# TensorE branches on each expert's token count: the last 64 rows of second parts left out where they are empty

## The chip, the cores and the metric

The kernel runs on one core of a Trainium2 chip. The metric is the device time of one execution in microseconds. PE is TensorE's matmul side and PEld its weight load, DVE is VectorE, ACT ScalarE, POOL GpSimd, SP SyncE. A letter q behind an engine's name (PEldq, SPq) marks what its sequencer does itself: branches, register loads, waits, DMA issues.

## What is computed

Three stages follow each other, in float32 from outside: a gated linear attention, a mixture of eight experts of which each token uses two, and a dense layer. Cut to what matters:

```python
# attention, per batch (4) and head (8), 768 steps, head size 48
state = f[:, :, t, :, None] * state + np.einsum('bhd,bhe->bhde', k[:, :, t], v[:, :, t])
y[:, :, t] = np.einsum('bhd,bhde->bhe', q[:, :, t], state)
# experts: 3072 tokens, 384 wide, 8 experts, 1024 hidden
logits = x @ w_gate
noisy_logits = logits + np.log1p(np.exp(x @ w_noise)) * noise
top2 = np.argpartition(-noisy_logits, 2, axis=1)[:, :2]
for e in range(E):
    for k in range(2):
        mask = top2[:, k] == e
        h = np.maximum(x[mask] @ w1[e], 0.0)
        out[mask] += top2_w[mask, k, None] * (h @ w2[e])
# dense: 2048 hidden
h = x @ w_in
return ((h - np.tanh(h)) @ w_out).astype(np.float32)
```

## The kernel before

Each expert has room for 832 tokens (CAP): the rows of its tokens are scattered to slots in DRAM (`xs`), the slots are loaded transposed (`load_x`), and two products run over them. The slots above an expert's token count are filled with zeros and computed all the same.

An expert's 832 slots are two parts, whose sizes `blocks(e)` gives: 320 and 512 for experts 0 and 7, 384 and 448 for expert 1, 512 and 320 for the others. Below, (5,1) is the second part of expert 5 and (5,0) its first. The hidden width is cut in eight, so a part has eight steps f. One step of a part is:

- `first_products`: nine matmuls with 128 hidden rows as the stationary side and the part's n tokens as moving columns (float16 high and low halves, three products for each of three 128-wide pieces of the input). The result, `ph`, is one PSUM bank.
- `moe_first` then lets ACT take the relu of it (hs, high half) and DVE the low half.
- `second_products`, two steps later (LAG = 2): for each 128 tokens of the part three matmuls with hs as the stationary side and 384 moving columns, into the banks b0, b1, b2, b5 (py). A rest of 64 tokens takes two matmuls, since its high and low halves stand side by side (`if m == 64`).
- after the last step `moe_second` lets ACT and DVE copy py out, and SP stores the rows to DRAM (`y_rows`).

The order of parts is written out by hand (`order`): (0,0) (1,0) (2,0) (0,1) (1,1) (2,1) (3,0) (3,1) (4,0) (4,1) (5,0) (5,1) (6,0) (7,0) (6,1) (7,1). In the trace (0,1) begins at 189 us, (2,1) at 249, (3,0) at 270, (5,1) at 403, (6,1) at 476, (7,1) at 496; the dense layer begins at 530. The main loop runs over n, the steps of all parts in that order, and puts other work in each step: weights of coming experts are loaded (`load_weights`) and split into high and low halves (`split_weights`, L155 on ACT and L156 on DVE), the dense layer's weights are decoded, the sums of squares of the weights are taken for a check (`weight_sum`, L161, on ACT: two per step in second parts), tokens of the first rows of the dense layer are gathered (`gather_y`, POOL) and combined. Each engine works off its own instructions in program order. At the end a flag decides whether a general fallback runs: every engine loads it (L1222) and branches on it (L1223); in the run shown the fallback's body is jumped over.

Of the kernel before, what the change touches and what calls it, by code (L numbers as in the profile page):

```python
# [26 lines left out]
FILLED = 640  # L27
Y_EARLY = (NE - 1) * CAP + 320


def blocks(e):
    cut = {0: 320, 1: 384, NE - 1: 320}.get(e, 512)
    return (0, cut), (cut, CAP - cut)


EARLY = {(0, 0): 12, (1, 0): 16, (2, 0): 20}
CLEARED = 16


# [35 lines left out]
def fast(ctx, tc, flag, f_cols, kq_cols, v_rows, gates, blank, void, w12, w_in, w_out, out):  # L75
# [102 lines left out]
    def load_x(e, blk, pieces):  # L178
        if pieces.start == 0:
            new_xt((e, blk))  # L180
        at, n = blocks(e)[blk]
        lo, hi = pieces.start * 128, min(n, pieces.stop * 128)
        if lo >= hi:
            return
        t = nc.sync.dma_start_transpose(XT[e, blk][:, :, lo:hi], xs[e * CAP + at + lo:e * CAP + at + hi, :])
        if (e, blk) in EARLY:
            early_rows[e, blk].append(t)
            for o in scatters[2 * EARLY[e, blk]:]:
                tc.declare_no_dep(t.ins, o.ins, reason="slots of late tokens are clamped to later rows")
# [7 lines left out]
    HS, PY = {}, {}  # L197
    def first_products(ph, n, lhs, key):
# [7 lines left out]

    def second_products(key, f, last, rhs, parts):
        hs = HS.pop((key, f))
        wh, wl = (w.rearrange("p a b -> p (a b)") for w in rhs)
        for i, (c0, m) in enumerate(parts):  # L210
            if f == 0:
                PY[key, i] = bank(f"py{i}", ("b0", "b1", "b2", "b5")[i])[:, :DM]
            p = PY[key, i]
# [7 lines left out]

    def moe_first(e, blk, f):
        n = blocks(e)[blk][1]
        w = RING[e, f]
        ph = bank("ph", next(tags["ph"]))
        first_products(ph, n, lambda a: (w[:, 0, a, :], w[:, 1, a, :]), (e, blk))
        hs = tiles.tile([128, 1024], F16, name="hs", bufs=4)
# [12 lines left out]

    def moe_second(e, blk, f):
        w = RING[e, f]
        second_products((e, blk), f, 7, (w[:, 0, 3:6, :], w[:, 1, 3:6, :]), parts(e, blk))
        if f < 7:
            return
        for i, (c, n) in enumerate(parts(e, blk)):
# [10 lines left out]
            nc.sync.dma_start(y_rows[at:at + n, :], y[:n])  # L257

    def pace(t):
        nc.gpsimd.tensor_copy(spacer, t)  # L260
# [9 lines left out]
    def moe_products(n):  # L270
        if n < len(moe_steps):
            moe_first(*moe_steps[n])
        if n >= LAG:
            moe_second(*moe_steps[n - LAG])

# [523 lines left out]
    def ff_second(blk, f):  # L799
        w = RING[NE, f // 2]  # L800
        c = 3 * (f % 2)
        second_products(("m", blk), f, 15, (w[:, 0, c:c + 3, :], w[:, 1, c:c + 3, :]),
                        [(128 * i, 128) for i in range(4)])
# [17 lines left out]
    for n in range(4, len(moe_steps) + LAG):  # L821
# [79 lines left out]
    def checks():  # L901
# [15 lines left out]
        nc.vector.tensor_scalar(total[:, 4:5], count[:, 4, NE - 1:NE], 320.0, None, op0=OP.is_le)  # L917
        holds(2, count[:, 0], float(CAP), OP.is_le)
# [363 lines left out]
```

## Time and profile before

| what | us |
|---|---|
| median of 3 runs | 910.54 (910.02 to 911.67) |
| the profiled execution | 914.9 |
| its span | 913.1 |
| PE busy | 896.9 |
| ACT busy | 604.7 |
| DVE busy | 576.8 |

The page's engine busy times are sums over the span; a matmul record is longer than the distance to the next one, as matmuls overlap in the array, so distances between starts tell what a matmul costs. The chain of waits follows the last instruction back to whatever released it.

### The profile page before, as it was taken

How to read it: one execution, taken by the hardware profiler on the slowest of the kernel's cores; microseconds unless marked ns; L12 is line 12 of the kernel's file. 1: busy time of each engine (PE TensorE's matmuls, PEld its weight loads, DVE VectorE, ACT ScalarE, POOL GpSimd, SP SyncE). 2: the span in 40 equal slices, each digit the busy share in tenths (PEclk: the TensorE clock that was granted, in tenths of full speed). 3: DMA queues.
4: the chain of work that ended last, by engine and by line, in shares of the span. 5: the costliest groups of instructions: out<-in, count | busy, mean ns of one | idle time of the engine just before them, and what ended most of it. 6: DMA issues, size and time to landing. Idle time of an engine off the chain costs nothing.

```text
span 913.1 us, 17400 instructions
## 1 busy us (share of the span) xinstructions
PE 896.9 (98%) x6422; PEld 531.0 (58%) x6422; DVE 576.8 (63%) x1167; ACT 604.7 (66%) x1560; POOL 173.8 (19%) x240
## 2 busy tenths in 40 slices
PE   8999899999999999999999999999999999999996
PEld 7888765555565656555566555555555555555553
DVE  7988866633467555666766756566465565565764
ACT  7989766455686656768658766666666666666652
POOL 3588834100000000000002132031140220320000
PEclk9999999999999999999999999999999999999999
DMA  8989999731568574646645722032031230330101
GB/s 246 204 256 288 277 283 313 215 99 53 153 199 217 136 190 116 181 126 170 159 137 121 191 71 61 10 96 44 18 98 25 61 70 10 79 58 4 36 1 39
DMA packets 112318, 116.58 MB, mean 128 GB/s; under 512 B 68208, under 2 KB 91376, under 8 KB 112080
## 3 DMA queue, kind: packets, MB, share of 16 engines
q1 hardware_dynamic: 105792, 96.11, 39.7%
q0 software_dynamic: 6144, 18.88, 7.0%
q8 instruction: 52, 0.85, 0.4%
q14 instruction: 42, 0.34, 0.1%
q10 hardware_dynamic: 288, 0.39, 0.1%
HBM read 72.88 MB, written 30.38 MB: 113 GB/s over the span
## 4 chain that ended last, share of the span: by engine, by line
PE 89%; DMA 5%; ACT 3%; issue 1%; DVE 1%; SPq 1%; POOL 0%; ACTq 0%; DVEq 0%
PE py L219 42%; PE ph L204 41%; PE pA L406 1%; PE pY L429 1%; DMA raw<-in_w 1%; DMA kq<-in_kq_cols 1%; PE pY L421 1%; DMA xt<-xs 1%; DMA f<-in_f_cols 1%; PE pX L472 1%; DMA v<-in_v_rows 1%; PE pkr L445 1%; PE pt L492 0%; ACT junk L161 0%; PE pK L458 0%
## 5 line engine op out<-in xcount | busy, mean ns | idle before, releaser
L219 PE MATMUL py<-wsplit,hs 128*128 128x384 f16 x2432 | 431.6, 326 | 1.4 <-DVE hs L796 0.6
L219 PEld LDWEIGHTS <-hs 128*128 128x128 f16 x2432 | 237.6, 98 | 172.7 <-DVE hs L796 0.9
L204 PE MATMUL ph<-xt,wsplit 128*128 128x512 f16 (+3 forms) x1152 | 223.5, 339 | 1.2 <-DMA xt<-xs 1.2
L204 PE MATMUL ph<-xt,winS 128*128 128x512 f16 x864 | 201.7, 379 | 0.0
L204 PEld LDWEIGHTS <-wsplit 128*128 128x128 f16 x1152 | 112.5, 98 | 87.5 <-issue 1.5
L787 DVE SCALAR_TENSOR_TENSOR s<-s,z 128x512 f32<-128x512 f32 x96 | 66.5, 692 | 138.9 <-ACT s L784 138.9
L237 DVE SCALAR_TENSOR_TENSOR hs<-ph,hs 128x256 f16<-128x256 f32 (+2 forms) x192 | 79.6, 443 | 113.6 <-ACT hs L229 111.8
L229 ACT ACTIVATE hs<-ph 128x512 f16<-128x512 f32 (+3 forms) x128 | 65.8, 514 | 118.5 <-PE ph L204 107.9
L783 ACT ACTIVATE z<-ph 128x512 f32<-128x512 f32 x96 | 57.3, 597 | 129.1 <-PE ph L204 129.1
L204 PEld LDWEIGHTS <-winS 128*128 128x128 f16 x864 | 84.4, 98 | 91.9
L156 DVE SCALAR_TENSOR_TENSOR wsplit<-raw,wsplit 128x768 f16<-128x768 f32 x72 | 68.8, 957 | 23.5 <-ACT wsplit L155 17.6
L161 ACT ACTIVATE junk<-wsplit 128x384 f16<-128x384 f16 x144 | 74.6, 518 | 2.7
L784 ACT ACTIVATE s<-z,bias_a 128x512 f32<-128x512 f32 x96 | 69.4, 723 | 3.1
L260 POOL CAST spacer<-hs 1x1 f32<-1x1 f16 x22 | 4.9, 222 | 343.0 <-ACT hs L229 342.5
L789 DVE SCALAR_TENSOR_TENSOR g<-s,ph 128x512 f32<-128x512 f32 x96 | 66.0, 687 | 6.1
L155 ACT ACTIVATE wsplit<-raw 128x768 f16<-128x768 f32 x72 | 60.0, 834 | 11.9 <-DMA raw<-in_w 10.7
L796 DVE TENSOR_TENSOR hs<-g,hs 128x512 f16<-128x512 f32 x96 | 65.7, 685 | 0.1
L260 POOL COPY spacer<-g 1x1 f32<-1x1 f32 x40 | 20.1, 502 | 224.0 <-DVE g L789 200.7
L795 ACT ACTIVATE hs<-g 128x512 f16<-128x512 f32 x96 | 58.9, 614 | 1.1 <-DVE g L789 1.1
L754 POOL DMA_INDIRECT g<-y_rows,yslot x48 | 51.4, 1070 | 18.6 <-issue 12.2
L574 POOL DMA_INDIRECT xs<-xkeep,yslot x48 | 50.8, 1059 | 16.5 <-issue 10.5
L390 POOL TENSOR_TENSOR kqT<-eneg,kq 128x512 f32<-128x512 f32 x23 | 29.5, 1285 | 15.5 <-ACT eneg L385 13.4
(146 smaller groups left out, 834.2 us busy)
## 6 DMA issues: line engine op xcount, KB each, us to landing
raw<-in_w SPq DMA_DIRECT2D x64, 384.0 KB
y_rows<-yo SPq DMA_DIRECT2D x48, 192.0 KB
kq<-in_kq_cols SPq DMA_DIRECT2D x42, 192.0 KB
w<-in_moe_w_out SPq DMA_DIRECT2D x32, 192.0 KB
w<-in_moe_w_in SPq DMA_DIRECT2D x24, 256.0 KB
v<-in_v_rows SPq DMA_DIRECT2D x24, 192.0 KB
out<-o SPq DMA_DIRECT2D x22, 192.0 KB
f<-in_f_cols SPq DMA_DIRECT2D x40, 96.0 KB
```

The costliest lines, as they stand in the source:

```text
L155: nc.scalar.activation(t[:, 0], raw, AF.Copy, scale=SW)
L156: nc.vector.scalar_tensor_tensor(t[:, 1], raw, SW, t[:, 0], op0=OP.mult, op1=OP.subtract)
L161: nc.scalar.activation(junk[:, :DM], RING[e, f][:, 0, 3 * i:3 * i + 3, :].rearrange("p a b -> p (a b)"), AF.Square, accum_out=wsum[:, 8 * ...
L204: nc.tensor.matmul(ph[:, :n], l, x[:, r, :n], start=(o == 0), stop=(o == 8))
L219: nc.tensor.matmul(p[:max(m, 128)], l, r, start=(f == 0 and o == 0), stop=(f == last and o == len(ops) - 1))
L229: nc.scalar.activation(hs[:, :n], ph[:, :n], AF.Relu, accum_out=hacc[:, at:at + 1])
L237: nc.vector.scalar_tensor_tensor(hs[:, at:at + hi - lo], ph[:, lo:hi], 0.0, hs[:, lo:hi], op0=OP.max, op1=OP.subtract)
L784: nc.scalar.activation(s, z, AF.Square, scale=1.0 / SZ, bias=bias_a)
L787: nc.vector.scalar_tensor_tensor(s, s, ZD, z, op0=OP.add, op1=OP.mult)
L789: nc.vector.scalar_tensor_tensor(g, s, 0.5, ph, op0=OP.mult, op1=OP.mult)
L795: nc.scalar.activation(hs[:, :512], g, AF.Copy)
L796: nc.vector.tensor_tensor(hs[:, 512:], g, hs[:, :512], op=OP.subtract)
```

## The change

The kernel counts the tokens of each expert on TensorE (six small matmuls over `owns`), DVE turns the counts into integers, and TensorE loads the eight counts into registers. In every step of a second part TensorE then branches: with more than 768 tokens (SHORT) it runs the old products, otherwise first products with 64 fewer columns and second products without the 64-row rest. Where the first and the second products of a step belong to the same expert's second part, one If holds both; there are 78 Ifs. Only TensorE has instructions in the bodies; relu, low halves, copies and stores work on the full part as before. Expert 7 is cut in 384 and 448 instead of 320 and 512. From the third part in `order` on, PSUM tiles are allocated once and kept (`lasting`), since both bodies have to write the same one. The weight sums of experts 2 to 6 are taken one per step in both parts instead of two per step in the second. The core of the diff:

```diff
-    cut = {0: 320, 1: 384, NE - 1: 320}.get(e, 512)
+    cut = {0: 320, 1: 384, NE - 1: 384}.get(e, 512)
+SHORT = CAP - 64
...
+    def either(e, emit):
+        if e is None:
+            emit(False)
+            return
+        with tc.If(many[e] > SHORT) as cond:
+            emit(False)
+        with cond.Else():
+            emit(True)
+
+    def products(first, second):
...
+            def emit_first(short):
+                w = RING[e, f]
+                first_products(ph, blocks(e)[blk][1] - (CAP - SHORT if short else 0),
+                               lambda a: (w[:, 0, a, :], w[:, 1, a, :]), (e, blk))
+
+            emits.append((e if blk else None, emit_first))
...
+            def emit_second(short):
+                w = RING[e2, f2]
+                done = parts(e2, blk2)
+                if short and done[-1][1] == CAP - SHORT:
+                    done = done[:-1]
+                second_products(hs, (e2, blk2), f2, 7, (w[:, 0, 3:6, :], w[:, 1, 3:6, :]), done)
+
+            emits.append((e2 if blk2 and parts(e2, blk2)[-1][1] == CAP - SHORT else None, emit_second))
+        if len(emits) == 2 and emits[0][0] == emits[1][0]:
+            either(emits[0][0], lambda short: [emit(short) for _, emit in emits])
...
+    def count_rows():
+        p = bank("pt", "b7")[:, :NE]
+        for g in range(NT // 4):
+            nc.tensor.matmul(p, ones, owns[:, g], start=(g == 0), stop=(g == NT // 4 - 1))
+        rows_of = consts.tile([1, NE], I32, name="rows_of")
+        nc.vector.tensor_copy(rows_of, p[0:1])
...
+        if n == 12:
+            rows_of = count_rows()
+        if n == 14:
+            take_rows(rows_of)
...
-        if blk == 1 and e < NE - 1:
-            weight_sum(e, f, 0)
-            weight_sum(e, f, 1)
+        if e < NE - 1:
+            for i in range(2) if e < 2 else (blk,):
+                if blk or e >= 2:
+                    weight_sum(e, f, i)
```

On PE, in (1,1), between the second products of one step and the first products of the next. Before (py with its numbers are the four banks of 128 tokens; the last has the 64-row rest):

```order
L219 MATMUL py_3463<-wsplit,hs 128x384
L219 LDWEIGHTS hs
L219 MATMUL py_3467<-wsplit,hs 128x384
L219 LDWEIGHTS hs
L219 MATMUL py_3467<-wsplit,hs 128x384
L204 LDWEIGHTS wsplit
L204 MATMUL ph<-xt,wsplit 128x448
```

Now, at the same place, the end of the body that runs with many tokens, with its jump, and the beginning of the other body:

```order
L236 MATMUL py_2905<-wsplit,hs 128x384
L236 LDWEIGHTS hs
L236 MATMUL py_2906<-wsplit,hs 128x384
L236 LDWEIGHTS hs
L236 MATMUL py_2906<-wsplit,hs 128x384
L275 UNCONDITIONAL_BRANCH
L217 LDWEIGHTS wsplit
L217 MATMUL ph<-xt,wsplit 128x384
```

The end of the other body, with its jump, and the branch of the next step:

```order
L236 LDWEIGHTS hs
L236 MATMUL py_2905<-wsplit,hs 128x384
L275 UNCONDITIONAL_BRANCH
L275 COMPARE_AND_BRANCH
L217 LDWEIGHTS wsplit
L217 MATMUL ph<-xt,wsplit 128x448
```

The short body ends with py_2905, the third bank, and its first products have 384 columns; the matmuls themselves stand in the same order as before, with a jump and a branch between two steps.

On ACT, two steps of (3,1). L229 is the relu, L232 a sum over the input, L161 the weight sums, L721 part of the decoding. Before:

```order
L229 ACTIVATE hs,hacc<-ph 128x320
L232 ACTIVATE junk,xsum<-xt 128x320
L161 ACTIVATE junk,wsum<-wsplit 128x384 x2
L229 ACTIVATE hs,hacc<-ph 128x320
L161 ACTIVATE junk,wsum<-wsplit 128x384 x2
L721 ACTIVATE wsq<-w_4168 128x192
```

Now (L243, L246, L163 and L793 are the same four lines):

```order
L243 ACTIVATE hs,hacc<-ph 128x320
L246 ACTIVATE junk,xsum<-xt 128x320
L163 ACTIVATE junk,wsum<-wsplit 128x384
L275 UNCONDITIONAL_BRANCH
L243 ACTIVATE hs,hacc<-ph 128x320
L163 ACTIVATE junk,wsum<-wsplit 128x384
L793 ACTIVATE wsq<-w_4443 128x192
```

One of the two sums of a step has gone to the same step of (3,0), and every If of PE leaves a jump on ACT, as it does on DVE, POOL and SP.

## Rows read from the trace of the kernel before

**Rows 1.** The page, busy us, share of the span, instructions of each engine.
```profile
PE 896.9 (98%) x6422; PEld 531.0 (58%) x6422; DVE 576.8 (63%) x1167; ACT 604.7 (66%) x1560; POOL 173.8 (19%) x240
```

**Rows 2.** The page, chain that ended last, share of the span by engine.
```profile
PE 89%; DMA 5%; ACT 3%; issue 1%; DVE 1%; SPq 1%; POOL 0%; ACTq 0%; DVEq 0%
```

**Rows 3.** The page's groups: line, operands, count; busy, mean ns; idle before, releaser.
```profile
L219 PE MATMUL py<-wsplit,hs 128*128 128x384 f16 x2432 | 431.6, 326 | 1.4 <-DVE hs L796 0.6
...
L204 PE MATMUL ph<-xt,wsplit 128*128 128x512 f16 (+3 forms) x1152 | 223.5, 339 | 1.2 <-DMA xt<-xs 1.2
L204 PE MATMUL ph<-xt,winS 128*128 128x512 f16 x864 | 201.7, 379 | 0.0
```

**Rows 4.** Timeline of PE, (0,1) and (2,1): start us, us, what, count.
```profile
216.43 2.10 PE L204 MATMUL ph<-xt,wsplit 128*128 128x512 f16 x9
218.38 2.11 PE L219 MATMUL py<-wsplit,hs 128*128 128x384 f16 x12
220.32 1.87 PE L204 MATMUL ph<-xt,wsplit 128*128 128x448 f16 x9
...
257.11 1.39 PE L204 MATMUL ph<-xt,wsplit 128*128 128x320 f16 x9
258.33 1.46 PE L219 MATMUL py<-wsplit,hs 128*128 128x384 f16 x8
259.63 1.39 PE L204 MATMUL ph<-xt,wsplit 128*128 128x320 f16 x9
```

**Rows 5.** Groups of PE by form, the counting matmuls of the final checks.
```profile
L911 PE MATMUL pt<-owns,ones 128*128 128x8 bf16 x19 | 0.6, 166 | 0.0
```

**Rows 6.** PE's register load of the flag (ns, start), and the timeline around it.
```profile
L1222 PEldq TENSOR_LOAD <-flag x1: 489/489/489, 902.4 to 902.4; - x1
```
```profile
901.37 4.07 PE L219 MATMUL py<-wsplit,hs 128*128 128x384 f16 x24
```

**Rows 7.** Line L1223: sequencer, operation, count, ns min/median/max, first and last start us.
```profile
L1223 POOLq COMPARE_BRANCH  x1: 45/45/45, 902.6 to 902.6; - x1
L1223 PEldq COMPARE_BRANCH  x1: 3842/3842/3842, 903.0 to 903.0; - x1
L1223 POOLq EVENT_SEMAPHORE  x1: 17/17/17, 903.1 to 903.1; - x1
L1223 DVEq COMPARE_BRANCH  x1: 72/72/72, 906.3 to 906.3; - x1
...
L1223 DVEq EVENT_SEMAPHORE  x1: 21/21/21, 910.2 to 910.2; - x1
```

**Rows 8.** Windows (2,1), (3,0), (5,1), (6,1): length; busy PE, PEld, DVE, ACT, POOL; PEclk, DMA share, GB/s.
```profile
248.57:270.36 21.79, 21.39 (x145) 13.73 (x143) 13.23 (x31) 17.10 (x53) 0.00 (x0) 1.00 0.63 178
270.36:300.82 30.46, 29.99 (x161) 15.64 (x160) 22.21 (x45) 21.03 (x56) 0.00 (x0) 1.00 0.74 203
...
403.46:424.94 21.48, 21.48 (x146) 14.09 (x144) 13.53 (x40) 17.82 (x64) 0.00 (x0) 1.00 0.65 165
...
476.26:496.44 20.18, 20.18 (x138) 13.31 (x136) 12.86 (x40) 17.61 (x63) 3.90 (x7) 1.00 0.50 120
```

**Rows 9.** Weight loads of the warm-up (timeline), and the waits of PE's sequencer on L204.
```profile
7.96 2.24 PEld L593 LDWEIGHTS <-ones 128*128 128x128 bf16 x40
```
```profile
L204 PEldq EVENT_SEMAPHORE  x18: 51/51/51, 133.3 to 833.2; - x18
```

**Rows 10.** Timeline of ACT in (5,1), two weight sums in a row.
```profile
412.38 0.52 ACT L161 ACTIVATE junk<-wsplit 128x384 f16<-128x384 f16 x1
...
413.03 0.52 ACT L161 ACTIVATE junk<-wsplit 128x384 f16<-128x384 f16 x1
```

**Rows 11.** Timeline of SP and PE where the dense layer begins.
```profile
523.03 1.22 SPq L770 DMA_TRANSPOSE xt<-m  x1
```
```profile
530.18 7.93 PE L204 MATMUL ph<-xt,winS 128*128 128x512 f16 x36
```

**Rows 12.** The page's DMA queues: packets, MB, share; the queue of PE's instructions.
```profile
q8 instruction: 52, 0.85, 0.4%
```

More of the change, by code (lines that the diff above doesn't have):

```diff
@@ L1 @@
 from contextlib import ExitStack
+from functools import partial
 from itertools import cycle
@@ L187, in load_x @@
             early_rows[e, blk].append(t)
+            for o in scatters[:2 * EARLY[e, blk]]:
+                tc.add_manual_dep(t.ins, o.ins.name, mybir.DependencyInfo(mybir.DependencyClass.Sync, mybir.DependencyReason.DATA),
+                                  reason="rows of earlier tokens")
             for o in scatters[2 * EARLY[e, blk]:]:
@@ L195, in bank, with lasting @@
         return (four if tag in ("b3", "b4", "b5", "b7") else ps).tile([128, 512], F32, name=name, tag=tag)
-    HS, PY = {}, {}
+    HS, PY, FIXED = {}, {}, {}
+    def lasting(e, blk, name, tag):
+        if order.index((e, blk)) < 2:
+            return bank(name, tag)
+        if tag not in FIXED:
+            FIXED[tag] = bank(name, tag)
+        return FIXED[tag]
     def first_products(ph, n, lhs, key):
@@ L205, in first_products, with begin_second, second_products @@
                 o += 1
-    def second_products(key, f, last, rhs, parts):
-        hs = HS.pop((key, f))
+    def begin_second(key, f, parts):
+        if f == 0:
+            for i in range(len(parts)):
+                new = bank if key[0] == "m" else partial(lasting, *key)
+                PY[key, i] = new(f"py{i}", ("b0", "b1", "b2", "b5")[i])[:, :DM]
+        return HS.pop((key, f))
+    def second_products(hs, key, f, last, rhs, parts):
         wh, wl = (w.rearrange("p a b -> p (a b)") for w in rhs)
         for i, (c0, m) in enumerate(parts):
-            if f == 0:
-                PY[key, i] = bank(f"py{i}", ("b0", "b1", "b2", "b5")[i])[:, :DM]
             p = PY[key, i]
@@ L220, in second_products, with relu @@
                                  stop=(f == last and o == len(ops) - 1))
-    def moe_first(e, blk, f):
+    def relu(e, blk, f, ph):
         n = blocks(e)[blk][1]
-        w = RING[e, f]
-        ph = bank("ph", next(tags["ph"]))
-        first_products(ph, n, lambda a: (w[:, 0, a, :], w[:, 1, a, :]), (e, blk))
         hs = tiles.tile([128, 1024], F16, name="hs", bufs=4)
@@ L239, in moe_first, with results @@
         HS[(e, blk), f] = hs
[L241 to L245, printed above, removed]
+    def results(e, blk):
         for i, (c, n) in enumerate(parts(e, blk)):
@@ L257, in moe_second, with moe_first @@
             nc.sync.dma_start(y_rows[at:at + n, :], y[:n])
+    many = []
+    def either(e, emit):
[7 more added lines that the diff above has]
+    def products(first, second):
+        emits = []
+        if first:
+            e, blk, f = first
+            ph = lasting(e, blk, "ph", next(tags["ph"]))
+            def emit_first(short):
[3 more added lines that the diff above has]
+            emits.append((e if blk else None, emit_first))
+        if second:
+            e2, blk2, f2 = second
+            hs = begin_second((e2, blk2), f2, parts(e2, blk2))
+            def emit_second(short):
[7 more added lines that the diff above has]
+            either(emits[0][0], lambda short: [emit(short) for _, emit in emits])
+        else:
+            for key, emit in emits:
+                either(key, emit)
+        if first:
+            relu(*first, ph)
+        if second and f2 == 7:
+            results(e2, blk2)
+    def moe_first(e, blk, f):
+        products((e, blk, f), None)
+    def moe_second(e, blk, f):
+        products(None, (e, blk, f))
     def pace(t):
@@ L270, in moe_products, with take_rows @@
     def moe_products(n):
[L271 to L274, printed above, removed]
+        products(moe_steps[n] if n < len(moe_steps) else None, moe_steps[n - LAG] if n >= LAG else None)
+    def count_rows():
[4 more added lines that the diff above has]
+        nc.vector.tensor_copy(rows_of, p[0:1])
+        return rows_of
+    def take_rows(rows_of):
+        _, values = nc.values_load_multi_w_load_instructions(
+            rows_of, engines=(mybir.EngineType.PE,), min_val=0, max_val=2 * N,
+            skip_runtime_bounds_check_because="the counts are only compared")
+        many.extend(values)
     with ExitStack() as actx:
```

7 lines of the change are left out of this document (4 added, 3 removed).

## The prediction

> **What bounds the kernel now.** I read the page's busy table first [rows 1]: PE is busy in 98% of the span, ACT in 66%, DVE in 63%. A busy PE can still hide waiting, so the chain of waits comes next [rows 2]: 89% of it is PE. The costliest groups close the question [rows 3]: in front of the 2432 second products (L219) PE sat idle for 1.4 us, in front of the 1152 first products of the experts (L204 with wsplit) for 1.2, in front of the 864 of the output stage for 0.0. That is 2.6 us in some 790. So the end is set by PE's own row of matmuls. Whatever shortens that row in the expert stage shortens the kernel, as long as PE is not made to wait.
>
> [...]
>
> **What is removed.** Which experts are short is a matter of data. From the reference's inputs I worked out the tokens per expert: 766, 738, 811, 777, 800, 755, 719, 778. At or below 768 (832 - 64) are experts 0, 1, 5 and 6: four take the short path, four (2, 3, 4, 7) the long one.
>
> First products: a group of nine matmuls is read as start to start of what follows [rows 4]: with 512 columns 218.38 - 216.43 = 1.95 us, with 320 258.33 - 257.11 = 1.22. Between them lie three steps of 64 columns, so each is worth 0.243 us. The four short experts run second parts of 512, 448, 320, 320, each in eight steps: 4 x 8 x 0.243 = 7.8 us. For 320 to 256 no row exists; I go on along the same line.
>
> Second products: twelve matmuls take 220.32 - 218.38 = 1.94 us, eight take 259.63 - 258.33 = 1.30 [rows 4], so 0.162 each. A 64-row rest costs two. Only experts 1, 5 and 6 have one in a second part (512 of expert 0 is four times 128): 3 x 8 x 2 x 0.162 = 7.8 us. **Removed: 15.6 us.**
>
> The new cut of expert 7 (384 and 448 instead of 320 and 512) brings nothing on these inputs: 832 columns either way, and 9 + 11 second matmuls instead of 8 + 12; with 778 tokens it takes the long path. One 64-row piece of it moves from (7,1) to (7,0), which leaves less time ahead of the output stage, dealt with below.
>
> **What is added on PE.** (1) The count: six matmuls of 8 columns, like the 19 of L911 that are busy for 0.6 us together [rows 5]: 0.2 us. (2) One load of eight registers. The trace has a load of one, on PE: 489 ns at 902.4 [rows 6]. While it ran, the array worked on a row of 24 matmuls that began at 901.37 and lasted 4.07 us [rows 6]; the load sat behind the last of them in program order. So PE's sequencer was 3.0 us ahead of the array (905.4 - 902.4), and the load was free. Eight times its time would be 3.9 us, 0.9 over that lead: 0 to 0.9, I take 0, as the row is of the very same operation. Queued behind it are only the next matmuls.
>
> (3) 78 branches on the count, each with one jump at the end of the body that runs. This is the term that decides, and before's trace shows only one branch, at the end of the kernel, over the long fallback: 45 ns on POOL, 72 on DVE, and 3842 ns on PE [rows 7]. DVE pays for the same far jump behind the record: its next instruction comes at 910.2, 3.8 us after its branch; POOL, which has little to jump over, goes on at 903.1, 0.45 us after. I read the 3.84 us on PE as the same fetch of far code, since it equals DVE's 3.8. The new jumps are short: they skip 13 to 41 instructions. For a short jump POOL's is the nearest row: 0.05 us for the record and at most 0.45 with what follows. Two per If are at most 1.0 us of sequencer time.
>
> Is that hidden? The lead is 3.0 us. Refilling it is quick: 40 loads and matmuls followed each other in 2.24 us [rows 9], so the sequencer can hand over a pair every 0.056 us. The tightest step is the shortened 256: 9 + 6 pairs, 0.98 + 0.98 = 1.95 us on the array, against 15 x 0.056 + 1.0 = 1.84 us on the sequencer. Further, the 18 waits that PE's sequencer runs alone on L204 (51 ns each) [rows 9] stand in front of first products, and in front of all 1152 of these lie the same 1.2 us, put down to a load of xt. So the bounds of what shows are 0 and 78 x 2 x 0.5 = 78 us; I take 0, nearest to these 18 rows and to the load.
>
> **What is moved.** Weight sums of experts 2 to 6: one per step in both parts instead of two per step in the second. A sum takes ACT 0.65 us, start to start (413.03 - 412.38) [rows 10]. So ACT loses 8 x 0.65 = 5.2 us in each of these second parts and gains it in the first parts. In (2,1) ACT is busy 17.10 of 21.79 us, and there and in (3,0) PE is idle for a moment: 21.79 - 21.39 = 0.40 and 30.46 - 29.99 = 0.47 us, behind hs and yo [rows 3, 8]; relief is worth up to 0.9. Against it, experts 0 and 1 end 6.5 us sooner in front of a stage where weight loads come late, which could cost the same. I take 0, with 0.9 either way. In (5,1) ACT is busy 17.82 of 21.48 [rows 8]; after, 12.6 of 16.9 (a short expert with a rest saves 1.95 + 2.6 = 4.5 us). Without that move ACT would not fit, so the move is the cover of the gain there. The first parts have room: (3,0), 21.03 of 30.46 [rows 8], becomes 26.2.
>
> Every other engine gets 78 unconditional jumps. On ACT they cost 0.05 to 0.07 us by the records, 0.5 by POOL's pause; ten of them in (5,1) are 0.5 to 5 us. At the upper end (5,1) has 17.6 us of ACT work in 16.9 and (6,1) 17.61 - 5.2 + 5 = 17.4 in 20.18 - 4.5 = 15.7: 2.5 us lost at most. I take 0, by the records.
>
> In the combined Ifs the signal to the relu comes two matmuls later, 0.33 us; its result is used two steps on, 3.9 us, so nothing waits. The first output product: its last transposed load is issued at 523.03, PE needs it at 530.18 [rows 11]. The rest of (7,1) behind it shrinks by about 0.9 us; the load still has 6 us.
>
> **Sum.** The profiled execution has a span of 913.1 us and took 914.9; the median of the runs shown is 910.54 (910.02 to 911.67). Durations in both are those of the same matmuls, so I take the difference to the median: 910.5 - 15.6 + 0.2 = 895.1, rounded up to 895.5 for losses of a few tenths that the bounds above allow.
>
> **Rivals.** *A branch on PE waits until the array is empty* (slower). For it: the 3842 ns record ends at 906.84, 1.4 us after the last matmul, and nothing of PE came between. Against: the load just ahead of it did not wait, and the number equals DVE's fetch. Price: an emptied pipe costs a matmul's record minus its spacing, 0.326 - 0.162 = 0.16, plus the branch of 0.05 to 0.07, so 0.23 per If at the least: 78 x 0.23 = 18, 913 us; with POOL's 0.5 in place of 0.07, 78 x 0.66 = 51, 947 us; at 1.4 each, 1004. It decides from 0.2 us per If on (15.6 / 78). *Jumps across a fetch boundary miss* (smaller gain): the page counts 52 instruction fetches for 2 x 6422 matmuls and loads [rows 1, 12], 247 instructions each; the bodies skipped on these inputs add up to 2098 instructions, so 8 to 9 jumps cross a boundary. Each shows 3.84 - 3.0 = 0.84 us: 7 us, 902.5. *ACT becomes the bound* by its own jumps: 2.5 us, 898. *The change does not do what it says*: with 766, expert 0 is two tokens off the limit; were it long, 1.9 us would be missing, 897.
>
> [...]
>
> **Chances.** Hidden branches with or without ACT's loss: 0.67 (893.5 to 898). Missed fetches or a part of the branches exposed: 0.13 (898 to 912; 0.09 of it below 908.7). Array emptied at each branch: 0.20 (912 to 1004). About 0.2% is what a measurement of this kernel can tell from no change. So faster 0.76, same 0.04, slower 0.20. The range runs from 893.5 (forecast less 0.9 for ACT's relief, and 1 of spread) to 912, where the first two cases end.
>
> **What would show it.** Right: in (5,1) and (6,1) groups of first products 0.98 us apart from what follows and second products 0.98, without idle time ahead of the first matmul of a body; no wait on PE labelled issue in the second parts. Wrong: idle time of 0.2 us or more in front of most bodies, in long experts too (the array empties); some eight waits of about a microsecond (fetches); or PE waiting for hs from ACT in (5,1) and (6,1).

## The result, and the profile after

| | us |
|---|---|
| before, median of 4 runs | 911.01 (910.02 to 911.67) |
| changed, median of 4 runs | 894.32 (894.05 to 895.43) |
| ratio, 95% interval | 0.982 (0.9803 to 0.9837) |
| profiled execution of the changed kernel, and its span | 894.53, 892.7 |

895.5 was forecast. Part of the difference of the two spans, 20.4 us, is not the change: the profiled execution of before was a slow one of its kind (914.9 beside a median of 911.0), and it lost its time ahead of (0,1). Over all profiles of this study (0,1) begins between 185.1 and 190.5 us, whatever was changed behind it. So stages are compared below by their own lengths, from the first matmul of one part to that of the next.

The page's busy row, its chain by engine, and its three groups of products (columns as in [rows 1 to 3], which they answer):

```profile
PE 881.0 (99%) x6380; PEld 525.8 (59%) x6380; DVE 574.9 (64%) x1167; ACT 601.7 (67%) x1561; POOL 173.8 (19%) x240
```

```profile
PE 91%; DMA 2%; ACT 2%; DVE 1%; POOL 1%; issue 1%; SPq 1%; DVEq 0%; POOLq 0%; ACTq 0%
```

```profile
L236 PE MATMUL py<-wsplit,hs 128*128 128x384 f16 x2384 | 423.9, 326 | 1.0 <-DVE hs L868 0.6
...
L217 PE MATMUL ph<-xt,wsplit 128*128 128x512 f16 (+4 forms) x1152 | 215.8, 333 | 0.0
L217 PE MATMUL ph<-xt,winS 128*128 128x512 f16 x864 | 201.7, 379 | 0.0
```

PE is 15.9 us less busy [rows 1], in 48 second products fewer (2432 to 2384: three experts, eight steps, two matmuls) and shorter first products. In front of the 1152 first products, of which the 576 of second parts now stand in bodies of Ifs, there is no idle time at all. In front of the second products of the experts there is one wait, 0.44 us for hs, and it stands inside a body and not at its start. So no body starts late, which answers the question on which the prediction turned.

Where two short steps of (5,1) follow each other, the timeline of PE (start, length, what, count) reads:

```profile
398.20 1.15 PE L217 MATMUL ph<-xt,wsplit 128*128 128x256 f16 x9
399.18 1.14 PE L236 MATMUL py<-wsplit,hs 128*128 128x384 f16 x6
400.16 1.15 PE L217 MATMUL ph<-xt,wsplit 128*128 128x256 f16 x9
401.14 1.14 PE L236 MATMUL py<-wsplit,hs 128*128 128x384 f16 x6
402.11 1.15 PE L217 MATMUL ph<-xt,wsplit 128*128 128x256 f16 x9
```

From start to start a group of nine with 256 columns takes 0.98 us and six second products 0.97: the line drawn from 512 and 320 columns [rows 4] holds down to 256, and no gap marks the branch at 398.20, 400.16 or 402.11.

The branches as PE's sequencer shows them (durations ns min/median/max, first and last start), all of the run, then those of (5,1), and the load of the counts:

```profile
L275 PEldq COMPARE_BRANCH  x118: 70/174/371, 181.9 to 508.9; - x118
```

```profile
L275 PEldq COMPARE_BRANCH  x8: 207/210/212, 392.7 to 408.7; - x8
```

```profile
L343 PEldq TENSOR_LOAD <-rows_of x1: 777/777/777, 149.1 to 149.1; - x1
```

118 records are the 78 branches and 40 more, one for each If that took its long body (ten each for experts 2, 3, 4 and 7): the jump over the short body. The jump that ends a short body leads to the next instruction and leaves no record. A short If shows about 0.21 us.

The records also tell how far ahead they run. The branch ahead of the body at 402.11 starts at 399.7: 2.4 us earlier, with some three of six second products, nine first and six second ones between, 18 matmuls. Of the others in (5,1), the one at 392.7 for the body at 395.27 and the one at 408.7 for that at 411.89 have 18 between as well, the one at 398.1 for 400.16 has 16. With wide matmuls this lead is worth over 3 us, in most tight steps 2.4. It is not always there: at eight of the 78 branches 4 to 13 matmuls were still to start, the least at the one at 488.2 in (7,1), 0.80 us ahead of its body. There hs had come only just in time (it was done at 486.98, and the second products that read it began at 487.20). These bodies follow without a gap too.

Lengths of stages in all runs, us, and the stretch from the start of (0,1) to the dense layer (pairs of starts of first products in each timeline of PE):

| run | (0,1) | (1,1) | (2,1) | (3,1) | (5,1) | (6,1) | (7,1) | stretch |
|---|---|---|---|---|---|---|---|---|
| before | 31.13 | 28.25 | 21.79 | 21.48 | 21.48 | 20.18 | 33.74 | 340.99 |
| changed | 29.22 | 24.37 | 20.51 | 21.49 | 17.61 | 16.63 | 30.06 | 325.06 |
| no branches | 29.22 | 24.38 | 21.07 | 21.48 | 17.61 | 16.64 | 29.87 | 324.83 |
| all long | 31.14 | 28.25 | 21.15 | 21.48 | 21.48 | 20.50 | 31.72 | 341.09 |
| all short | 29.22 | 24.37 | 19.38 | 17.61 | 17.62 | 16.64 | 29.90 | 314.26 |
| 376 Ifs | 29.22 | 28.13 | 21.67 | 21.48 | 21.41 | 20.60 | 31.62 | 339.31 |
| 1072 Ifs | 29.22 | 41.79 | 55.27 | 44.26 | 36.68 | 35.76 | 68.26 | 500.12 |
| 126 more skipped | 29.22 | 24.37 | 20.51 | 21.48 | 21.65 | 19.30 | 32.46 | 333.69 |
| 522 more skipped | 29.22 | 24.38 | 20.50 | 21.48 | 44.03 | 37.85 | 31.47 | 375.09 |
| sums put back | 29.22 | 24.38 | 20.50 | 21.48 | 17.61 | 16.64 | 31.26 | 326.35 |
| cut put back | 29.22 | 24.37 | 20.51 | 21.48 | 17.62 | 16.31 | 33.58 | 325.23 |
| finer | 29.22 | 24.37 | 22.66 | 20.52 | 17.80 | 16.08 | 32.31 | 326.70 |
| finer, 3 to 6 | 29.22 | 24.37 | 20.51 | 20.53 | 17.61 | 15.67 | 30.35 | 322.14 |

The stretch is 15.9 us shorter than before, 15.6 were forecast. The parts of long experts, (3,1) and (4,1), which also branch in every step, kept their length to 0.01 us.

### The profile page after: what moved, and what is told of

It reads as the page before. It is cut to its first block, busy times and chain, and to the rows that moved or that the text cites. A ratio compares the mean times of both kernels' runs of the same rounds, so it can differ in the third digit from the quotient of the medians.

```text
span 892.7 us, 17436 instructions
## 1 busy us (share of the span) xinstructions
PE 881.0 (99%) x6380; PEld 525.8 (59%) x6380; DVE 574.9 (64%) x1167; ACT 601.7 (67%) x1561; POOL 173.8 (19%) x240
## 4 chain that ended last, share of the span: by engine, by line
PE 91%; DMA 2%; ACT 2%; DVE 1%; POOL 1%; issue 1%; SPq 1%; DVEq 0%; POOLq 0%; ACTq 0%
PE py L236 43%; PE ph L217 41%; PE pY L501 2%; PE pA L478 2%; PE pY L493 1%; PE pkr L517 1%; DMA kq<-in_kq_cols 1%; PE pX L544 1%; DMA v<-in_v_rows 1%; DMA raw<-in_w 1%; POOL kqT L462 1%; PE pt L564 1%; PE pK L530 1%; POOL xs L646 0%; DVE wsplit L158 0%
## 5 line engine op out<-in xcount | busy, mean ns | idle before, releaser
L236 PE MATMUL py<-wsplit,hs 128*128 128x384 f16 x2384 | 423.9, 326 | 1.0 <-DVE hs L868 0.6
L236 PEld LDWEIGHTS <-hs 128*128 128x128 f16 x2384 | 232.7, 98 | 167.7 <-DVE hs L251 1.2
L217 PE MATMUL ph<-xt,wsplit 128*128 128x512 f16 (+4 forms) x1152 | 215.8, 333 | 0.0
L243 ACT ACTIVATE hs<-ph 128x512 f16<-128x512 f32 (+3 forms) x128 | 65.8, 514 | 99.7 <-PE ph L217 80.9
L158 DVE SCALAR_TENSOR_TENSOR wsplit<-raw,wsplit 128x768 f16<-128x768 f32 x72 | 68.8, 956 | 26.7 <-ACT wsplit L157 26.1
L163 ACT ACTIVATE junk<-wsplit 128x384 f16<-128x384 f16 x144 | 74.1, 514 | 1.4
```

Of the source, the lines that this page charges most:

```text
L158: nc.vector.scalar_tensor_tensor(t[:, 1], raw, SW, t[:, 0], op0=OP.mult, op1=OP.subtract)
L163: nc.scalar.activation(junk[:, :DM], RING[e, f][:, 0, 3 * i:3 * i + 3, :].rearrange("p a b -> p (a b)"), AF.Square, accum_out=wsum[:, 8 * ...
L217: nc.tensor.matmul(ph[:, :n], l, x[:, r, :n], start=(o == 0), stop=(o == 8))
L236: nc.tensor.matmul(p[:max(m, 128)], l, r, start=(f == 0 and o == 0), stop=(f == last and o == len(ops) - 1))
L243: nc.scalar.activation(hs[:, :n], ph[:, :n], AF.Relu, accum_out=hacc[:, at:at + 1])
```

## The experiments

The question of the prediction was whether a branch on PE costs the array time. Two theories stood: branches are covered by the sequencer's lead over the array; or each costs the array something (0.16 us for an emptied pipe, or less). "No branches", "the changed kernel again", "all long" and "sums put back" stand beside the same runs of before (median 910.84); 376 Ifs, 1072 Ifs, 522 more and all short beside others (912.53), 126 more, the cut and the finer version beside a third set (911.41).

**No branches.** Which experts are short is fixed in the program, right for these inputs alone; everything else stays.

```diff
-        with tc.If(many[e] > SHORT) as cond:
-            emit(False)
-        with cond.Else():
-            emit(True)
+        emit(e in (0, 1, 5, 6))
```

> The changed kernel with its 78 branches taken out: which experts are short (0, 1, 5, 6) is fixed when the kernel is built; count, register load and all other moves stay. My theory, that the branches are covered because the sequencer of PE is some 18 matmuls ahead of the array: the same time as with branches, 894.3 within 0.9. Rival, that each branch costs a little in the array: the difference divided by 78 is the price of one If; at the 0.16 us of an emptied pipe 894.3 - 12.5 = 882.

894.56 us, ratio to before 0.9821 (0.9805 to 0.9837). **The changed kernel again**, beside it:

> The changed kernel once more, beside its variants: 894.3 within 0.9.

894.92, ratio 0.9823 (0.9808 to 0.9839). The 78 branches cost nothing that can be measured. Stage by stage the run without branches and the changed kernel agree within 0.6 us, both ways.

**All long.** The branches and the other moves, with no product saved.

```diff
-        with tc.If(many[e] > SHORT) as cond:
+        with tc.If(many[e] > 8) as cond:
```

> The changed kernel with the limit at 8 tokens instead of 768, so that all 78 Ifs run their long body: the branches and the moves without any saving. Theory of covered branches: the time of the kernel before, 911.0, plus 0.2 for the count, less up to 0.9 for relief of ACT: 910.3 to 911.3. A price per If of 0.05 us would give 915, of 0.16 us 924.

910.98, ratio 1.0002 (0.9991 to 1.0012), stretch 341.09 against 340.99. The interval is one us to either side, 0.015 us for an If, and (3,1) and (5,1), which have eight to ten Ifs each and no wait, kept their 21.48 to the hundredth. Inside the stretch two differences cancel, and the waits of PE put neither down to a branch: (2,1) and (3,0) are 1.1 us shorter together than before, whose waits for hs and yo are gone, and (7,0), (6,1) and (7,1) 1.2 longer, with 0.76 us of waiting for hs in (7,1). The rival with an emptied array, 0.16 us for each, is out for these Ifs.

**376 Ifs and 1072 Ifs.** To see whether the cover has an end, the bodies were cut into Ifs of three matmuls, then of one (range step 3, then 1).

```diff
+        for lo in range(0, count, 3):
+            some = range(lo, min(lo + 3, count))
+            with tc.If(many[e] > SHORT) as cond:
+                emit(False, some)
+            if lo < few:
+                with cond.Else():
+                    emit(True, some)
```

> The changed kernel with 376 Ifs instead of 78: each If holds three matmuls instead of a whole product. In the trace of the changed kernel a short If shows one branch record of 0.21 us, a long one two of 0.07 and about 0.2. A step of expert 5 has 15 matmuls and five Ifs then: 15 x 0.056 + 5 x 0.21 = 1.9 us of sequencer against 1.96 us of array; one of expert 3 17 and six: 0.95 + 1.6 = 2.6 against 2.52. Theory of covered branches: at the edge, 894.3 to 897. A price in the array of 0.16 us per If: 298 more Ifs, 942.

> The changed kernel with 1072 Ifs: each holds one matmul and its weight load. Theory: now the sequencer is the bound. Per matmul 0.056 + 0.27 us in long bodies and 0.056 + 0.21 in short ones, against 0.11 to 0.17 in the array: some 3 us more in each long step of experts 2, 3, 4 and 7, 2 us in each of 1, 5 and 6, about 1040 in all, with idle time marked issue in front of most matmuls of second parts. If the cover held whatever the number: 894.3.

With three matmuls in each: 912.05 us, 17 more than the changed kernel (14 in the stretch), and 15 over the end of what I had expected. The stages say where. Long bodies stayed free, (3,1) is 21.48 as before with six Ifs in most steps. The short bodies of experts 1, 5 and 6 did not, those of expert 0 did. Two steps of (5,1), and what PE's sequencer did in that part:

```profile
411.36 1.16 PE L218 MATMUL ph<-xt,wsplit 128*128 128x256 f16 x9 [0.46 <-PEq L279]
412.36 1.14 PE L238 MATMUL py<-wsplit,hs 128*128 128x384 f16 x6
414.04 1.16 PE L218 MATMUL ph<-xt,wsplit 128*128 128x256 f16 x9 [0.55 <-PEq L279]
```

```profile
L279 PEldq COMPARE_BRANCH  x36: 202/208/320, 403.5 to 420.5; - x36
L279 PEldq EVENT_SEMAPHORE  x5: 51/51/51, 408.3 to 418.8; - x5
```

A step takes 414.04 - 411.36 = 2.68 us instead of 1.96 (2.43 to 2.68 in the six like it), and PE waits for its own sequencer (PEq, at the line of the Ifs). There are six Ifs in it, not the five that I counted: the rest of 64 rows is an If of its own, with nothing behind its Else. This If is the cause, and not the number of Ifs. In each step in which its body is skipped, PE's sequencer waits once for a semaphore (EVENT_SEMAPHORE), 24 times in all, three experts in eight steps; and these are the waits of PE (total us, times, longest):

```profile
L279 PEldq EVENT_SEMAPHORE  x24: 51/51/51, 227.9 to 502.5; - x24
```

```profile
PE ph L218 <- PEq L279: 9.5, 22, 0.6
```

By the trace the semaphore is one that PE's own matmuls raise, and each of the 24 records begins 0.04 us after that of the last matmul has ended: the array has run empty. With the two shortest waits (0.15 us each) the idle time is 9.8 us, and by the prediction's estimate (a matmul's record less its spacing, 0.326 - 0.162) the emptied pipe costs 0.16 more each time, 3.9 together: 13.7 of the 14.2 us. The changed kernel has no such wait at its 78 Ifs, which all have an Else with matmuls in it. The branches of the five other Ifs of a step follow each other at 0.29 us where nothing holds them up, three matmuls included. That is 1.4 us for the five, less than the 1.96 of the array. So this run does not show where the cover ends. A cut into as many Ifs without the empty Else was not run.

With one matmul in each: 1073.53 (about 1040 was expected). Windows of (3,1) and (5,1) of this run, columns as in [rows 8]:

```profile
345.28:389.54 44.26, 41.29 (x146) 14.25 (x144) 12.16 (x39) 12.36 (x47) 0.00 (x0) 0.77 0.35 90
493.53:530.21 36.68, 31.35 (x133) 13.15 (x132) 14.65 (x43) 14.72 (x53) 0.00 (x0) 0.72 0.39 105
```

Here the sequencer is the bound. Where a long body stands in every If, as in (3,1), branch follows branch after 0.38 to 0.39 us, with one matmul in each, and a matmul has 0.14 to 0.16 us of the array. Short ones follow each other after 0.28, and two rests in each step, skipped one behind the other, empty the array as above (48 such records). Both kinds of stage are some 20 us longer, and the granted clock was 0.77 and 0.72 in these two windows, where (5,1) had 1.00 before [rows 8]. (0,1) is unchanged even here: its nine first products (448 columns) are in Ifs, 9 x 0.28 = 2.5 us, beside twelve plain second products, in a step of 3.65 us. So the cover is a matter of sums over a few steps: matmuls of array time on one side, and on the other 0.28 us for a short If and 0.38 for a long one, the first matmul of its body included. For further matmuls 0.056 us each [rows 9] is more than enough: three instead of one in a short If made 0.29 of 0.28. A short step of 1.96 us has room for some (1.96 - 0.84) / 0.28 = 4 Ifs by this estimate, and the change uses one.

**Longer jumps.** My second rival was the jump to code not yet fetched. The skipped long body of the first products of (5,1) and (6,1) was made longer by copies that never run, 522 instructions, then 126 (range 30, then 8).

```diff
-                first_products(ph, blocks(e)[blk][1] - (CAP - SHORT if short else 0),
+                for _ in range(30 if blk and e in (5, 6) and not short else 1):
+                    first_products(ph, blocks(e)[blk][1] - (CAP - SHORT if short else 0),
```

> The changed kernel with a longer jump: in the first products of (5,1) and (6,1), whose short body runs, the long body that is skipped is made 522 instructions longer (29 more copies of the nine matmuls), 16 Ifs in all. What is executed stays the same. Theory that a jump to code not yet fetched costs a fetch, as at the end of the kernel before (3.84 us): 3.84 less the 2.4 us that the sequencer is ahead there, 1.4 for each of 16: 917. Rival, that only the number of branches counts and not their length: 894.3.

> As the run with 29 more copies in the skipped bodies of (5,1) and (6,1), but with seven: 8 copies of nine matmuls, so 126 instructions more, 16 Ifs. If the cost grows with the length of the jump: 126 / 522 of 52.9 us, 12.8, so 907. If it is a matter of code not yet fetched, and what lies within one fetch ahead (247 instructions by the count of fetches) is there already: 894.5 to 896.

522 more: 947.23, 52 us above the changed kernel, not 23. 126 more: 903.73, 9 above, between the two expectations. PE's waits of both kernels (what for; total us, times, longest), first 522 then 126:

```profile
PE ph L217 <- issue: 32.5, 15, 4.9
```

```profile
PE ph L217 <- issue: 6.0, 4, 2.2
```

And the timelines of PE around such jumps, 522 then 126:

```profile
402.23 2.08 PE L217 MATMUL ph<-xt,wsplit 128*128 128x256 f16 x9 [4.91 <-issue]
404.11 2.85 PE L236 MATMUL py<-wsplit,hs 128*128 128x384 f16 x12
406.79 1.15 PE L217 MATMUL ph<-xt,wsplit 128*128 128x256 f16 x9
```

```profile
404.27 0.82 PE L217 MATMUL ph<-xt,wsplit 128*128 128x256 f16 x6
406.58 0.49 PE L217 MATMUL ph<-xt,wsplit 128*128 128x256 f16 x3 [1.49 <-issue]
...
408.86 1.14 PE L236 MATMUL py<-wsplit,hs 128*128 128x384 f16 x6
```

The instruction queues of the pages (packets, MB, share), 522 then 126; the changed kernel has 60 and before 52 [rows 12]:

```profile
q8 instruction: 89, 1.46, 0.7%
```

```profile
q8 instruction: 68, 1.11, 0.5%
```

The branches of (5,1), 522 then 126:

```profile
L275 PEldq COMPARE_BRANCH  x8: 3321/4774/5380, 390.8 to 429.9; - x8
```

```profile
L275 PEldq COMPARE_BRANCH  x8: 212/268/4685, 392.8 to 412.8; - x8
```

With 522 instructions more each of the 16 branches took 3.3 to 5.4 us instead of 0.2, and PE waited 15 times, 2.2 us each on the mean. Most of the rest of the 50 us I put down to the clock (15 emptied pipes make some 2.4, by the 0.16 above): behind such a wait nine matmuls take 1.88 us from start to start (404.11 - 402.23) instead of 0.98, and the granted clock of (5,1) is 0.78. The jumps went over 8352 more instructions, 34 fetches at 247 each, and 29 more fetches were made: nearly all of the code is fetched though it is jumped over.

With 126 more, well within one fetch, PE waited four times. Where, the trace's transfers of PE's instruction queue tell: in (5,1) they start at 394.4, 399.9, 404.3 and 409.8. The last two took 0.93 and 0.96 us, so they landed at 405.3 and 410.8, and PE went on at 406.58 and 412.16, each 1.3 to 1.4 us behind the landing. The first of these two waits stands inside a group, behind six of its nine matmuls, so I take it to be the boundary between two fetches that PE waits at there, not a branch. The second wait is at a branch, whose record runs from 407.4 for 4.69 us, and so are the two in (6,1), with records of 3.17 and 3.69. From the start of a fetch to the first matmul out of it pass 2.3 us, about the sequencer's lead. By the same 2.3 us the fetch of 399.9 comes due at 402.2, where the sequencer is late already (the group starts at 402.30, 0.05 behind the one before it), and that of 394.4 falls under the wide second products and shows nowhere. I read this as a matter of how fast the code is gone through: a fetch every 10 us is no trouble in (5,1) of the changed kernel (394.2 and 404.4), one every 4 to 5.5 is. No run separates this from where in a fetch a jump stands. The remaining 2 us of this run are in (7,1), by waits for hs: 0.7 behind gathered rows and 1.4 behind a load of the dense layer's weights, both of which "All short" shows below.

**Sums put back.** One move undone.

```diff
-        if e < NE - 1:
-            for i in range(2) if e < 2 else (blk,):
-                if blk or e >= 2:
-                    weight_sum(e, f, i)
+        if blk == 1 and e < NE - 1:
+            weight_sum(e, f, 0)
+            weight_sum(e, f, 1)
```

> The changed kernel with one move undone: the weight sums of experts 2 to 6 again two per step in second parts. My step said that without the move ACT (17.8 us busy in (5,1) before, some 0.5 more with ten jumps) does not fit in the stage, now 17.6 us long, nor its 18.1 in (6,1), now 16.6: 0.7 + 1.5, so 896.5, with PE waiting for hs in (6,1). Rival, that what ACT falls behind is caught up in the next first part while PE works on: 894.3.

896.71, 1.8 above the changed kernel beside it, and near the 896.5 expected; but not in the place. (5,1) and (6,1) did not grow by more than 0.01 us. Windows of (5,1), (6,1) and (7,1) of this run (ACT is the fourth busy number):

```profile
393.82:411.43 17.61, 17.61 (x134) 12.92 (x132) 12.36 (x36) 15.44 (x56) 0.00 (x0) 1.00 0.70 161
...
464.99:481.63 16.64, 16.64 (x129) 12.33 (x126) 10.87 (x33) 14.79 (x54) 2.36 (x4) 1.00 0.54 126
481.63:512.89 31.26, 30.36 (x174) 16.67 (x173) 24.09 (x55) 24.52 (x64) 7.84 (x13) 1.00 0.61 162
```

and of the changed kernel:

```profile
392.33:409.94 17.61, 17.61 (x134) 12.91 (x132) 13.04 (x38) 14.14 (x51) 0.00 (x0) 1.00 0.69 169
...
463.51:480.14 16.63, 16.63 (x127) 12.31 (x126) 11.88 (x36) 13.08 (x47) 3.84 (x7) 1.00 0.56 137
480.14:510.20 30.06, 30.05 (x175) 16.73 (x173) 22.98 (x52) 22.07 (x55) 6.29 (x10) 1.00 0.59 163
```

ACT fell behind in (5,1), where its relu starts up to 1.8 us after the first products end instead of 0.04, and was on time again from the third step of (6,0) on, while PE never waited. In (6,1) it did not get through its work either and carried some 2.5 us into (7,1) (24.52 against 22.07). There PE waited 0.45 us for a copy of py out by ACT, and a little more behind it:

```profile
489.30 0.65 PE L236 MATMUL py<-wsplit,hs 128*128 128x384 f16 x3 [0.45 <-ACT yo L265]
490.11 1.46 PE L236 MATMUL py<-wsplit,hs 128*128 128x384 f16 x8 [0.16 <-DVE yo L263]
```

These and one more of 0.29 us make 0.9 of the 1.2 by which (7,1) is longer. The other 1.0 us of PE idle in this profile lies in (1,0), ahead of anything the edit touches. In (3,0) the wait for yo that before had (0.47 us) is back, with 0.54; in no run with the sums moved is it longer than 0.1.

**Cut put back.** Expert 7 in 320 and 512 again.

```diff
-    cut = {0: 320, 1: 384, NE - 1: 384}.get(e, 512)
+    cut = {0: 320, 1: 384, NE - 1: 320}.get(e, 512)
```

> The changed kernel with the new cut of expert 7 undone (320 and 512 again). By my step it is nothing on these inputs, as expert 7 has 778 tokens and runs long bodies: the same columns, and 8 + 12 second products instead of 9 + 11, so (7,0), (6,1) and (7,1) add up to 70.9 us either way, and the time stays 894.3 to 894.9. Rival, that the cut is worth a wait in front of the dense layer: 1 us either way in (7,1).

895.06, ratio 0.9821 (0.9807 to 0.9834), stretch 325.23. Nothing, as predicted: (7,0) is 2.9 us shorter than in the changed kernel and (7,1) 3.5 longer, and the three stages (7,0), (6,1) and (7,1) take 71.4 us instead of 71.1.

**All short.** How far the gain goes when every expert is short. On these inputs the kernel then leaves out the tokens above 768 of experts 2, 3, 4 and 7, so it is a probe of time alone.

```diff
-        with tc.If(many[e] > SHORT) as cond:
+        with tc.If(many[e] > 4000) as cond:
```

> The changed kernel with the limit at 4000 tokens, so that all Ifs run their short body; experts 2, 3, 4 and 7 lose their tokens above 768. By the terms of the prediction: first products 8 x 8 x 0.243 = 15.6 us less than before, second products 7 x 8 x 2 x 0.162 = 18.2, so 911.0 - 33.8 + 0.2 = 877.4. Rival, that ACT, DVE or a load of weights becomes the bound when all second parts shrink: 879 or more, with PE idle in front of hs or of weight loads in the second parts.

888.88, beside runs of before with a median of 912.53; 877.4 was expected by the terms, 879 by that median. Two things ate the difference. What is left after the second, some 3 us, must lie outside the stretch; (0,1), ahead of which there are no Ifs, begins at 190.5 in this profile, and at 187.5 to 189.1 in the three others beside it. In the stretch the gain is 26.7 us instead of 33.8: (3,1), (4,1), (5,1) and (6,1) shrank in full, (2,1) and (7,1) did not. Timeline of PE, then of DVE, in (7,1):

```profile
493.24 0.49 PE L236 MATMUL py<-wsplit,hs 128*128 128x384 f16 x2
495.90 1.31 PE L236 MATMUL py<-wsplit,hs 128*128 128x384 f16 x7 [2.17 <-DVE hs L251]
```

```profile
492.24 0.62 DVE L833 SCALAR_TENSOR_TENSOR g<-g,wt,g 128x384 f32<-128x384 f32 x1 [3.89 <-DMA g<-y_rows,yslot]
492.78 0.95 DVE L158 SCALAR_TENSOR_TENSOR wsplit<-raw,wsplit 128x768 f16<-128x768 f32 x1
...
495.29 0.68 DVE L251 SCALAR_TENSOR_TENSOR hs<-ph,hs 128x384 f16<-128x384 f32 x2
```

DVE stands 3.89 us in front of rows gathered for the dense layer; six instructions later it makes the low half for which PE then waits 2.17 us. A second wait of 1.5 us, at 502.7, comes from ACT, which stood 1.44 us in front of a load of the dense layer's weights. So the next bound of (7,1) is this gather and this load, and in (2,1), where PE waits 2.1 us for hs, it is the load of the next expert's weights (ACT stands 2.18 and 1.53 us in front of it), seen next.

**Finer.** With the branches free, a second If inside each body takes the first products to 832, 800, 768 or 736 tokens.

```diff
+                with tc.If(many[e] > SHORT + 32) as inner:
+                    emit(0)
+                with inner.Else():
+                    emit(32)
...
-                first_products(ph, blocks(e)[blk][1] - (CAP - SHORT if short else 0),
+                first_products(ph, blocks(e)[blk][1] - less,
```

> A finer version: in the combined steps a second If inside each body leaves out 32 columns more of the first products, so that they are done for 832, 800, 768 or 736 tokens. Experts 3, 4 and 7 (777, 800, 778) have then 32 columns less, expert 6 (719) too: 4 x 8 x 0.122 = 3.9 us less than the changed kernel, 890.4 to 891. Two Ifs a step take some 0.6 us of sequencer beside 0.84 for its matmuls, under the 1.84 of the array, so they stay covered. Rivals: PE waits in (7,1) for DVE, as it does where all bodies are short: 1 us of it lost; or the second If is not covered: up to 0.3 us in each of some 60 steps, 894.5 + 14.

894.66 (892.86 to 896.73), ratio 0.9816 (0.9799 to 0.9833): no gain. (3,1) and (4,1) shrank by 0.97 and 0.83 us, near the 0.97 worked out, so the second Ifs are covered, but two branch records of 2.24 and 2.38 us, which I read as code that came late, cost PE 0.12 us in (4,1) and 0.40 in (6,1), and (5,1) is 0.19 longer. And (2,1) and (7,1) each grew by over 2 us. ACT in (2,1), then PE behind it:

```profile
254.50 0.84 ACT L157 ACTIVATE wsplit<-raw 128x768 f16<-128x768 f32 x1 [4.79 <-DMA raw<-in_w]
...
256.02 0.41 ACT L243 ACTIVATE hs<-ph 128x320 f16<-128x320 f32 x1
```

```profile
256.58 0.50 PE L236 MATMUL py<-wsplit,hs 128*128 128x384 f16 x2 [0.76 <-ACT hs L243]
258.12 1.15 PE L236 MATMUL py<-wsplit,hs 128*128 128x384 f16 x6 [1.05 <-DVE hs L251]
```

ACT waits 4.79 us for a load of the coming expert's weights, and the relu is queued behind it. In the changed kernel the longest such wait in this stage is 2.3 us. (7,1) waits as it did with all bodies short, 0.6 us behind the gather and 1.8 behind the load of the dense layer's weights. Of the spread of five runs, 3.9 us, loads that come now early, now late, would be a cause; I did not test it.

**Finer, experts 3 to 6.** The second Ifs only where no transfer stands in the way.

```diff
-            either(emits[0][0], lambda less: [emit(less) for _, emit in emits], True)
+            either(emits[0][0], lambda less: [emit(less) for _, emit in emits], emits[0][0] in (3, 4, 5, 6))
```

> The finer version with its second Ifs for experts 3 to 6 alone, so that (2,1) and (7,1), where the finer version showed PE waiting for hs behind loads of weights and gathered rows, are as in the changed kernel. If the second Ifs are covered and those two stages were the whole loss: (3,1) 0.96, (4,1) 0.83 and (6,1) 0.55 us shorter than in the changed kernel as the finer version showed, and (2,1) 20.5 and (7,1) 30.1 again, so some 2.3 less than the changed kernel: 892.0 to 892.6. If what is gained earlier is only waited for later, in front of the dense layer: 894.3 to 894.9, with (7,1) longer by what the others lost.

893.21 (892.59 to 897.1), ratio 0.9775 (0.9752 to 0.9798); the median lies above the 892.6 that ended the first expectation, but the runs of before beside it were higher too (914.44), so the medians say less than the stages. The stretch of the one profile is 322.14, 2.9 us under the changed kernel: (3,1), (4,1) and (6,1) are each 0.96 shorter, and (2,1) and (7,1) are where they were within 0.3. By the stages the first expectation holds, and by its ratio to before this is the best complete version run.

## Why the prediction was right, step by step

- *What is removed.* 15.6 us was predicted, the stretch lost 15.9. (0,1): 1.91 of 1.94. (5,1) and the start of (6,0): 3.87 + 0.65 of 4.55. (7,0), (6,1) and (7,1) together 4.33 of 4.55. (1,1) and (2,1) 5.16 of 4.54: 0.40 of the excess is the wait for hs in (2,1), which the prediction named and took at nothing. It is not gone but has moved: (3,0) now has one of 0.44 for hs, while its own of 0.47, which was for yo, is gone. So the relief of ACT that the prediction took at 0, with up to 0.9, is small: (2,1) and (3,0) together take 51.05 us with the sums put back, and 50.96 and 50.63 in the two runs of the changed kernel. The wait for hs changes from run to run (none to 0.44 us).
- *Count and load.* The six matmuls took 0.15 us of PE (0.2 predicted). The load of eight registers took 777 ns, not eight times the 489 of one; nobody waited.
- *Branches.* Taken as hidden; they are, to 0.015 us each on the mean and better in the stages without waits. The way there had wrong numbers that did no harm, which is in part luck. The lead is not 3.0 us: it is a row of some 16 to 18 matmuls, 2 to 3.5 us with their width, and where the sequencer has waited itself down to 0.80. The 0.056 us for a pair is no price of the sequencer: in the run with 376 Ifs three pairs fit in the 0.08 us between the end of one branch and the start of the next. And an If costs the sequencer 0.28 to 0.38 us, not up to 1.0. The tightest step has therefore 1.96 us of array against some 1.1 of sequencer (0.84 + 0.28), more room than the 1.84 that I allowed.
- *The emptied array*, chance 0.20, did not happen: all bodies of all 78 Ifs follow without a gap, and 78 branches without savings time as before. It does happen at an If without an Else, 24 and 48 times in the runs with 376 and 1072 Ifs. The one branch in the trace of before, at its end, has no Else either, and the same kind of record follows it on PE's sequencer (at 906.9 us), so it was a poor stand-in for the new ones.
- *Missed fetches*, chance of 0.13 with its like: its count was right, eight fetches more (60 against 52), its price was not: at jumps of 13 to 41 instructions they show nowhere, and no branch of the 78 took more than 0.37 us. With longer jumps they do, at some 3 us for each of 16, nearly a third of it, by my estimate, by the clock (0.78 in (5,1)), where I had worked out 0.84 (in the experiment 1.4) from the far jump of [rows 7]: that jump is paid once, these come in a row. The margin is not wide, for the finer version, with no copies, already has two such records.
- *Weight sums as cover.* The step said that (5,1) would not fit without the move. It fits: ACT falls behind there and catches up in (6,0). The stages are also longer than the step took them, 17.61 and 16.63 us instead of 16.9 and 15.7, as part of the saving lies two steps later in the next part, and ACT was busy 14.14 in (5,1) after the move, not 12.6. The move is worth 1.8 us all the same, of which the profile shows 1.2 in (7,1), where PE waits for copies of py behind what is left over from (6,1). That the run came near its 896.5 is luck, for that number stood for waits in (5,1) and (6,1).
- *ACT's jumps* at up to 0.5 us each: no stage shows them, and in every step of (5,1) the relu starts 0.04 us behind the last first product. Nor does the signal to it come two matmuls later, as the prediction had it. *The recut*: nothing, as said.
- *The sum* came to 895.1, rounded up to 895.5 for small losses; 894.32 and 894.92 were measured. Of the missing 0.6 to 1.2, some 0.4 is the rounding and some the waits in (2,1) and (3,0); the rest is within what the stage ahead of (0,1) changes from run to run.

## What to carry to other kernels

The 78 branches on a register cost PE at most 0.015 us each, as its sequencer stayed ahead: compare, over a step, the matmuls' array time with the 0.28 to 0.38 us that an If took here, its first matmul included, and at most 0.056 for each further pair. Give every If an Else with work in it, for here a skipped body without one made PE wait for its own last matmul, 24 times in the run with 376 Ifs. Keep what is jumped over short, for here 522 instructions more in each of 16 skipped bodies meant 29 fetches more, where 34 would hold all of them, and a stretch 50 us longer. Load the register well ahead: here it was read 33 us before its first use, and a later load was not tried. When a stage shrinks, look for what was just fast enough there: here loads of weights, for which ACT stood up to 4.79 us, and a gather, for which DVE stood 3.89, each ahead of work that PE waited for, gave back the next 4 us.

## What the hardware showed that I had not expected

- PE's sequencer ran a number of matmuls ahead, 16 to 18 with their weight loads (32 to 36 instructions) where it had not waited itself, in short and in wide steps, and not a fixed time: 2 to 3.5 us.
- The same If cost differently by its path: a long one 0.07 us for the branch and 0.17 or more for the jump, 0.38 from If to If with one matmul in it; a short one 0.21 for the branch and 0.28 from If to If.
- Stalls in fetching cost more than their idle time: in the run with 522 more, 32.5 us of idle time went with a stretch 50 us longer, and with a granted clock of 0.78 in (5,1).
- An If without an Else, with its body skipped, made PE's sequencer wait until the array had run empty: 24 waits, 9.8 us of idle time, in the run with 376 Ifs.
